# Linear attention mixed with a two-dimensional DFT on one core: transposes in pairs of q' tiles, and operand forms made at other places

## The chip, the cores and the metric

The kernel runs on 1 core of one Trainium2 chip. The metric is the device time of one execution in microseconds (us); the time before is the median of 3 runs. TensorE is called PE, its weight load PEld, VectorE DVE, ScalarE ACT, GpSimd POOL and SyncE SP, as in the profile.

## The reference

Everything is fp32, with S = 2048 rows and D = 576 columns in H = 32 heads of 18.

```python
def _A_ref(x, wqkv, wo):                       # linear attention
    q, k, v = (x @ wqkv) split into three, each into 32 heads
    phi = lambda t: where(t > 0, t + 1, exp(t)) + 1e-6
    pq, pk = phi(q), phi(k)
    kv  = einsum("bhsd,bhse->bhde", pk, v)
    z   = einsum("bhsd->bhd", pk)
    num = einsum("bhqd,bhde->bhqe", pq, kv)
    den = einsum("bhqd,bhd->bhq", pq, z)[..., None] + 1e-6
    return (num / den) joined to (1, S, D) @ wo

def _B_ref(x, dft_seq_re, dft_seq_im, dft_hid_re, dft_hid_im):
    a = x @ dft_hid_re.T ; b = x @ dft_hid_im.T
    return dft_seq_re @ a - dft_seq_im @ b

g = sigmoid((x * gate_w).sum(-1, keepdims=True))
out = g * _A_ref(x) + (1 - g) * _B_ref(x)
```

## The kernel before

**Products.** Every fp32 operand is split into a `hi` and a `lo` part (`hi_of` on ACT, L173, rounds; `lo_of` on DVE, L183, takes the difference), and a product is three matmuls: hi·hi, hi·lo, lo·hi. The last 64 of the 576 columns ("the rest") are packed with their lo into one set of 128 partitions, so a tile of 128 rows against 288 columns takes 14 matmuls, and both halves 28.

**Stages, in PE's order.** (1) k': x times Wk, 16 tiles of 128 rows; the first four run together, the other twelve one after another (`k_half`, L203). The features phi are made by ACT (exp) and DVE (L367), and k' is kept split as `pk`. (2) k'^T x (L676): 20 steps of up to 24 matmuls, each step on one chunk of `xg`, a copy of x in another layout, loaded by SP into a ring of 4 buffers (`cs_ring`, L578) and split by ACT and DVE. After every fourth step `kv_step` (L658, L661) multiplies by Wv. (3) q': 16 tiles (`q_tile`) of x times Wq, which also give the gate's logit; DVE makes the features into `acc[i]`, and 1 + exp(−logit) is inverted with two DVE operations of 128x1 for each tile (L736, L737). Between them M = kv·Wo is built (`build_m`, `split_m`), and `normalise` divides each pair of tiles by its denominators (L749 to L757) and copies the rest columns twice beside each other (`twice`, L762). (4) The attention loop: each normalised tile is transposed by PE, four times 128x128 of `acc` and once `twice` (`transposed`, L779), the transposes are split by ACT and DVE out of PSUM into `qs`, and 28 matmuls (L203) with M give the tile, which ACT evicts with the gate as scale (L1164). (5) The DFT along D (L945) and along S (L1099) in two rounds, each made of seven products of a fast scheme.

**Operand forms for the DFT.** The seven products need sums and differences of blocks of x (left sides) and of the hidden DFT matrix (right sides). `Left(k, ...)` loads a block pair of x (L383, or L389 for the last, k = 8) over POOL's DMA queue, `make` takes two DVE additions twice, the hi on ACT, the lo on DVE, and stores to `xm` in HBM (L408). The last left side is kept for six stores of its rest (`store_rest`, SP). `right(wr, ...)` does the same for three pieces of Wr: load (L435), eight additions on DVE in two steps, hi on ACT (128x2016), lo on DVE (128x1152 and 128x864), store to `wm`. All of this is cut into generators, and `go(gen, n)` puts the next n steps at a chosen place.

**What sets the order.** ACT, DVE and SP run in the order in which the program writes their instructions, from k' on (`manual_schedule`). POOL is ordered by the scheduler, and so is PE until the hidden DFT begins. The tiles of x for k' and q' come by SP into a ring (`load_next`) and are split by `split_next` two tiles ahead. PSUM has 8 banks.

Of the kernel before, what the change touches and what calls it, by code (L numbers as in the profile page):

```python
# [78 lines left out]


PRODUCTS = {1: (4, 0), 6: (2, 4), 2: (6, 1), 5: (1, 3), 7: (0, 5), 3: (3, 2), 4: (5, 6)}
ORDER = (3, 2, 7, 6, 1, 4, 5)
# [49 lines left out]
def kernel(  # L132
# [108 lines left out]

    acc = [at(ACC_AT + i * D * 4, [P, D], F, "acc") for i in range(NT)]

# [130 lines left out]
    class Left:  # L374
# [3 lines left out]
        def __init__(self, k, start, after):  # L378
            self.k = k
            if k < NP:  # L380
                self.f, self.c = (at(start, [P, 7, 2, 2 * P], d, "xb") for d in (F, R))
                for i in range(2):
                    begin_after(nc.gpsimd.dma_start(out=self.f[:, 4 * i + 1:4 * i + 3, 1],  # L383
                                                    in_=xq[k, :, 2 * i:2 * i + 2]), after)
                return
            raw, self.plain = (at(start, [P, 2, 2, 7, P], d, "xb") for d in (F, R))
            self.f, self.c = (t.rearrange("p g a f n -> p f a g n") for t in (raw, self.plain))
            for i in range(4):
                begin_after(nc.gpsimd.dma_start(  # L389
                    out=self.f[:, (1, 2, 5, 6)[i], 1],  # L390
                    in_=xq[k, :, i].rearrange("p (g n) -> p g n", g=2)), after)

# [22 lines left out]
    def store_rest():  # L415
        t = rest_stores.pop()
        for k in range(3):
            for g in range(2):
                nc.sync.dma_start(out=xrest_of[g, k], in_=t[:, g, k // 2])

    def left_part():
# [159 lines left out]
    def xg_next(lo_of=lo_of):  # L581
        if xg_raw:
# [6 lines left out]
            xg_split.append(t)  # L589

    for i in range(FT, NT):
        xs = split.pop(0)
        k_half(i, 0, xs)
        if FT < i < NT - 2:
# [9 lines left out]
        if 8 <= i < 12:  # L604
            xg_load()
        if i < NT - 1:
            load_next()
# [59 lines left out]
    for c in range(5):  # L667
        ps = [bank(), bank()]
        passes = FULL if c < KC else FULL[:2]
        for q in range(NCU):  # L670
# [13 lines left out]
            if step in (1, 2):  # L684
                split_next(lo_later)
            if q == 1 and c:
# [5 lines left out]
            if step == 0:  # L692
                add(zacc, acc[0], acc[1])
            elif step < NT - 1:
                add(zacc, zacc, acc[step + 1])
            if step == NT + 1:
# [20 lines left out]
        gt = gts[c] = at(gt_ring.next(), [P, 2, D], R, "gt")  # L717
# [7 lines left out]
    def q_tile(i):  # L725
        xs = split.pop(0)
        if i == 0:
            split_next()
# [7 lines left out]
        nc.vector.tensor_scalar(g, g, 1.0, None, op0=ALU.add)  # L736
        nc.vector.reciprocal(out=g, in_=g)  # L737
        load_next()
        if i:
            split_next()  # L740

    pz_ring = Ring(T_AT + 40960, D * 4, 4)

    def normalise(k):
# [10 lines left out]
        for i in range(2):  # L755
# [6 lines left out]
            nc.vector.tensor_copy(out=twices[-1],  # L762
                                  in_=rest.unsqueeze(1).to_broadcast([P, 2, REST]))
            yield

    twices = []
    norms = (part for k in range(NT // 2) for part in normalise(k))


    qs_ring = Ring(T_AT + 50176, XS, 2)  # L770

    def transposed(i):

        xs, _ = new_xs("qs", qs_ring)
        banks = [bank(), bank()]
        twice = twices.pop(0)
        for c in range(5):
            a = acc[i][:, c * P:(c + 1) * P] if c < KC else twice.rearrange("p a b -> p (a b)")
            nc.tensor.transpose(banks[c // KC][:, (c % KC) * P:(c % KC + 1) * P], a, ident)  # L779
        hi_of(xs[:, 0:4], banks[0])  # L780
        lo_of(xs[:, 5:9], banks[0], xs[:, 0:4])
        hi_of(xs[:, 4], banks[1][:, :P])
        lo_of(xs[:, 9], banks[1][:, :P], xs[:, 4])
        return xs

# [5 lines left out]
    mraw = at(T_AT + 23040, [P, KC, D], F, "mraw")  # L791
    mrest = at(T_AT + 32256, [P, D], F, "mraw")

    def build_kv():
# [40 lines left out]
    def split_m(h):  # L835
        hi_of(mhi[:, :KC, half(h)], mraw[:, :, half(h)])
        lo_of(mlo[:, :, half(h)], mraw[:, :, half(h)], mhi[:, :KC, half(h)])
        hi_of(mhi[:, KC, half(h)], mrest[:, half(h)])
        lo_of(mhi[64:, KC, half(h)], mrest[64:, half(h)], mhi[64:, KC, half(h)])

    def m_row(h, j):
        return mhi[:, j, half(h)] if j <= KC else mlo[:, j - 5, half(h)]

    store_rest()
    wr_forms, wr_pieces = right(wr, wr_rest, ((0, T_AT + 60416), (1, T_AT + 76544),
                                              (2, T_AT + 60416)))
    xs_ring.at[3] = T_AT + 105664
    load_next()
    q_tile(0)
    for f in wo_split:  # L850
        f()
    kv_step(4)
    q_tile(1)
    build_kv()
    q_tile(2)
    next(norms)
    q_tile(3)
    go(wr_pieces[0])
    next(norms)
    build_m((0, 1))  # L860
    for i in range(4, NT):
        q_tile(i)
        build_m({4: (2, 3), 5: (4,)}.get(i, ()))
        for g in range(2 * (i - 4), min(2 * (i - 3), NG)):
            move_m(g)
        for k, j, n in ((0, 4, 2), (0, 5, 1), (0, 6, 2), (1, 4, 1), (1, 7, 2), (1, 8, 1),
                        (1, 11, 2), (2, 9, 1), (2, 13, 2), (2, 14, 1)):
            if i == j:
                go(wr_pieces[k], n)
        if i in (5, 8, 11, 12, 13):  # L870
            go(norms)
        if i == NT - 3:
            nxt = transposed(0)
        if i in (9, 10):
            split_m(i - 9)

# [182 lines left out]
    def sequence(m, g, src, dst, last=None, between=None):  # L1059
# [91 lines left out]
    made = {}  # L1151
    plan = {
        2: [(0, 1)], 3: [(0, 1)], 4: [(0, 1)], 5: [(0, 1)], 6: [(0, 1)], 7: [(1, 1)], 8: [(1, 1)],
        9: [(1, 1)], 10: [(1, 1)], 11: [(1, 1)], 12: [(7, 1)], 13: [(7, 1)], 14: [(7, 1)],
        15: [(7, 2)],
    }
    for i in range(NT):
        qs = nxt
        if i + 1 < NT:
            nxt = transposed(i + 1)  # L1160
        for h in range(2):
            ps = bank()
            run(ps[:, :HALF], steps(qs, lambda j: m_row(h, j)))
            done.append(nc.scalar.activation(acc[i][:, half(h)], ps[:, :HALF], AF.Copy,  # L1164
                                             scale=gate[:, i:i + 1]))
        nc.gpsimd.dma_start(out=att[i], in_=acc[i])
        go(norms, 2)
        if i == 0:
            go(wr_pieces[2], 2)
        for k, n in plan.get(i, ()):  # L1170
            go(made[k], n)
        for k, j, o in ((0, 0, SLOT_AT), (1, 3, SLOT_AT + 7 * XF),
                        (NP - 1, 8, T_AT + (NP - 2) * TPAIR)):
            if i == j:
                left = Left(k, o, done[-1])
                made[k] = left.make()
                if k < 2:
                    hidden.take_x(k, left.c)
        if i == 7:
# [4 lines left out]
        for p, j in ((1, 8), (2, 11), (3, 15)):  # L1184
            if i == j:
                hidden.load_rest(p)
        if i == 11:
            hidden.load_pair(2)
        if i in (13, 15):
            for k in (0, 2) if i == 13 else (4, 6):  # L1190
                hidden.load_x(3, k)
    nc.vector.tensor_scalar(gate_n, gate, -1.0, 1.0, op0=ALU.mult, op1=ALU.add)
# [34 lines left out]

    paced.enter_context(tc.manual_schedule(engines={mybir.EngineType.PE}))
    first.load_rest(4)
# [96 lines left out]
```

## Time and profile before

| | |
|---|---|
| median of 3 runs | 726.98 us (726.65 to 727.15) |
| the profiled execution | 726.5 us, span 724.8 us |
| granted TensorE clock | 1.0 throughout |
| busy: PE, DVE, ACT, POOL | 719.7, 600.5, 334.7, 57.2 us |
| chain that ended last | PE 94%, DMA 3%, DVE 1% |
| HBM | 115.05 MB read, 41.39 MB written, 216 GB/s |

Stages by PE's timeline, in us of the span: k' until 64.5, k'^T x until 129.5, q' until about 195 (the first transposes are at 183.6), the attention loop until 262.8, hidden DFT until 314.8, sequence DFT until 491.9, the second round until 718, and a tail until 724.8.

How to read the rows: the busy rows give us, share of the span and number of instructions; a group's row has "busy, mean ns of one" and the idle time before its instructions with what ended it; a chain's row has its start, its length and what it is; in a timeline's row stand start and length of a run of instructions and, in brackets, the idle time before it. L numbers are lines of the kernel before.

### The profile page before, as it was taken

Reading aid. Unit: us, or ns where it says so; the run is one execution under the profiler, and the core shown is the slowest. Engines: PE = TensorE matmul, PEld = TensorE weight load, DVE = VectorE, ACT = ScalarE, POOL = GpSimd, SP = SyncE. Lnnn points to the kernel's source line nnn. Section 1 sums busy time; section 2 is a strip of 40 time slices with the busy share of each in tenths; the row PEclk is TensorE's granted clock in tenths of the full one; section 3 lists DMA queues with packets and bytes.
Section 4 is the critical chain, followed back from the end, with each engine's and each line's share of the span. In section 5 each row is a group of like instructions: output and inputs, shape, how many; then the busy total and the mean of one; then the engine's idle time right before and its main releaser. Section 6 shows DMA issues by size and latency. Waiting matters only on the chain.

```text
span 724.8 us, 13886 instructions
## 1 busy us (share of the span) xinstructions
PE 719.7 (99%) x5444; PEld 718.8 (99%) x5444; DVE 600.5 (83%) x995; ACT 334.7 (46%) x522; POOL 57.2 (8%) x98
## 2 busy tenths in 40 slices
PE   9999999999999999999999999999999999999998
PEld 9999999999999999999999999999999999999997
DVE  5789867689999948989999999767889987788884
ACT  5998335688644444543433334323535432232231
POOL 1011300051032210000010000000000000000000
PEclk9999999999999999999999999999999999999999
DMA  7376795676477989744475576889963543454440
GB/s 256 88 276 220 267 338 174 245 218 223 158 218 296 352 311 375 243 158 127 144 265 187 164 280 205 291 307 398 376 219 134 171 154 131 124 178 153 153 153 33
DMA packets 54372, 158.82 MB, mean 219 GB/s; under 512 B 6436, under 2 KB 11108, under 8 KB 53284
## 3 DMA queue, kind: packets, MB, share of 16 engines
q1 hardware_dynamic: 45060, 118.90, 48.6%
q0 software_dynamic: 8960, 38.65, 14.6%
q8 instruction: 43, 0.70, 0.4%
q10 hardware_dynamic: 288, 0.39, 0.1%
q14 instruction: 21, 0.17, 0.1%
HBM read 115.05 MB, written 41.39 MB: 216 GB/s over the span
## 4 chain that ended last, share of the span: by engine, by line
PE 94%; DMA 3%; DVE 1%; POOL 0%; ACT 0%; issue 0%; SPq 0%; DVEq 0%; ACTq 0%; POOLq 0%
PE bank L1099 48%; PE bank L203 23%; PE bank L945 14%; PE bank L676 3%; PE bank L520 2%; PE bank L779 1%; DMA craw<-in_xg_dram 1%; DMA xm<-xb 1%; DMA wraw<-in_wv_dram 1%; PE bank L229 1%; POOL xb L389 0%; PE bank L658 0%; ACT xb L173 0%; DVE row L1115 0%; SPq L311 0%
## 5 line engine op out<-in xcount | busy, mean ns | idle before, releaser
L1099 PE MATMUL bank<-fh,c 128*128 128x288 f32 x1792 | 354.7, 294 | 0.0
L1099 PEld LDWEIGHTS bank<-fh,c 128*128 128x128 f32 x1792 | 286.7, 188 | 0.0
L1099 PE MATMUL bank<-fl,c 128*128 128x288 f32 x896 | 263.6, 294 | 0.0
L173 ACT ACTIVATE c<-craw 128x1792 fp32r<-128x1792 f32 (+1 forms) x84 | 121.3, 1448 | 181.4 <-DVE craw L193 153.6
L1099 PEld LDWEIGHTS bank<-fl,c 128*128 128x128 f32 x896 | 168.7, 188 | 0.0
L183 DVE TENSOR_TENSOR c<-craw,c 128x1792 fp32r<-128x1792 f32 (+4 forms) x86 | 142.0, 1654 | 6.8 <-ACT c L173 6.7
L193 DVE TENSOR_TENSOR craw<-craw 128x256 f32<-128x256 f32 (+1 forms) x192 | 98.0, 512 | 21.4 <-DMA craw<-in_ci_dram 11.5
L203 PE MATMUL bank<-wd,xs 128*128 128x288 f32 (+1 forms) x784 | 105.9, 296 | 0.0
L203 PEld LDWEIGHTS bank<-wd,xs 128*128 128x128 f32 x784 | 104.6, 188 | 0.1
L945 PE MATMUL bank<-wf,xf 128*128 128x288 f32 x588 | 91.1, 295 | 0.0
L945 PEld LDWEIGHTS bank<-wf,xf 128*128 128x128 f32 x588 | 83.4, 189 | 0.0
L203 PE MATMUL bank<-mw,qs 128*128 128x288 f32 x448 | 63.2, 297 | 0.0
L676 PE MATMUL bank<-pk,c 128*128 128x288 f32 x448 | 61.2, 296 | 0.3 <-ACT c L173 0.3
L676 PEld LDWEIGHTS bank<-pk,c 128*128 128x128 f32 x448 | 59.9, 189 | 0.7 <-ACT c L173 0.5
L203 PEld LDWEIGHTS bank<-mw,qs 128*128 128x128 f32 x448 | 59.9, 188 | 0.2 <-DVE qs L183 0.2
L367 DVE SCALAR_TENSOR_TENSOR acc<-bank,e 128x288 f32<-128x288 f32 x64 | 28.2, 453 | 20.1 <-ACT e L366 14.9
L193 DVE TENSOR_TENSOR ys<-bank,ys 128x288 f32<-128x288 f32 x63 | 28.8, 457 | 15.5 <-PE bank L1099 12.5
L183 DVE TENSOR_TENSOR fl<-fl,fh 128x864 fp32r<-128x864 f32 (+1 forms) x32 | 34.5, 1093 | 6.5 <-ACT fh L173 5.3
L173 ACT ACTIVATE fh<-fl 128x864 fp32r<-128x864 f32 (+1 forms) x32 | 29.8, 950 | 16.6 <-DVE fl L193 15.4
L945 PE MATMUL bank<-wf,xr 96*128 96x288 f32 x112 | 33.3, 298 | 0.0
L1164 ACT ACTIVATE acc<-bank,gate 128x288 f32<-128x288 f32 x32 | 16.0, 502 | 35.1 <-PE bank L203 34.8
L193 DVE TENSOR_TENSOR ys<-ys,bank 128x288 f32<-128x288 f32 x47 | 21.2, 450 | 13.3 <-PE bank L1099 12.8
(107 smaller groups left out, 664.6 us busy)
## 6 DMA issues: line engine op xcount, KB each, us to landing
xf<-xm SPq DMA_DIRECT2D x42, 512.0 KB, 9.0
craw<-in_cr_dram SPq DMA_DIRECT2D x32, 512.0 KB, 3.7
craw<-in_ci_dram SPq DMA_DIRECT2D x32, 512.0 KB, 3.7
xraw<-in_xa_dram SPq DMA_DIRECT2D x28, 320.0 KB, 3.9
xm<-xb POOLq DMA_DIRECT2D x8, 1024.0 KB, 6.7
wf<-wm SPq DMA_DIRECT2D x14, 576.0 KB, 5.3
xr<-xr SPq DMA_DIRECT2D x14, 448.0 KB, 8.5
xm<-xb POOLq DMA_DIRECT2D x8, 768.0 KB, 6.7
```

The lines of the kernel that those rows point to most:

```text
L173: return nc.scalar.activation(dst, src, AF.Copy, bias=bias)
L183: nc.vector.tensor_tensor(out=dst, in0=src, in1=hi, op=ALU.subtract)
L193: nc.vector.tensor_tensor(out=dst, in0=a, in1=b, op=op)
L203: nc.tensor.matmul(ps, a, b, start=(n == 0), stop=(n == len(pairs) - 1))
L229: nc.tensor.matmul(warm[:, :P], ones_f, ones_f, start=True, stop=True)
L367: nc.vector.scalar_tensor_tensor(dst, ps, 0.0, e, op0=ALU.max, op1=ALU.add)
L520: nc.tensor.matmul(ps[i][h], x[:, i * P:(i + 1) * P], wkt.row(h, j), start=(c == 0 and n == 0), stop=(c == KC and n == 1))
L676: nc.tensor.matmul(ps[h][:, :HALF], t[:, a, k], pk[s][:, b, half(h)], start=(s == 0 and n == 0), stop=(s == NT - 1 and n == len(passes) - 1))
L779: nc.tensor.transpose(banks[c // KC][:, (c % KC) * P:(c % KC + 1) * P], a, ident)
L945: nc.tensor.matmul(ps, a, b, start=(start and n == 0), stop=(n == len(ops) - 1), skip_group_check=True)
L1099: nc.tensor.matmul(ps[q], c[x][:, l, k], factors[p](y, f), start=(p == 0 and i == 0), stop=(p == NP - 1 and i == 2))
L1164: done.append(nc.scalar.activation(acc[i][:, half(h)], ps[:, :HALF], AF.Copy, scale=gate[:, i:i + 1]))
```

## The change

1. `transposed` now takes a pair of tiles: 4 transposes of 128x128 for each, and one for the rest columns of both (`last`, one copy per pair instead of `twice` for each). Of that last bank, each tile's 64 rows go as hi by ACT to their own partitions and as lo by DVE to the other 64; M's rest has its lo in a tile of its own, `mlast`, 128 partitions wide. The matmuls stay 28 for each tile. PE follows the written order from the attention loop on.
2. The gate's two operations are done once over 128x16, ahead of the attention loop.
3. q' runs in the order `TURNED`: x tiles 12, 13, 14 first, whose splits are kept from k', then 15, 0, 1 to 11. Three loads of x and three splits go.
4. Piece 1 of Wr is made during k' (tiles 4 to 11), piece 0 during k'^T x (steps 13 to 19), piece 2 during q'.
5. x's sides: left side 7 is made between q' tiles 6 and 15 instead of in the attention loop, sides 0 and 1 start one iteration later, and the last left side (8) is loaded by SP at step 6 of k'^T x, into another place; its rest stores go out two at a time after q' tiles 0, 1 and 2. The sum of k' over the tiles (`zacc`) runs from the last tile to the first.
6. `xg` has 5 buffers, and step 0 of k'^T x issues two loads.
7. The norms run earlier among the q' tiles, and loads for the hidden DFT in the attention loop stand at other iterations.

```diff
-            for i in range(4):
-                begin_after(nc.gpsimd.dma_start(
-                    out=self.f[:, (1, 2, 5, 6)[i], 1],
-                    in_=xq[k, :, i].rearrange("p (g n) -> p g n", g=2)), after)
+                nc.sync.dma_start(out=self.f[:, (1, 2, 5, 6)[i], 1],
+                                  in_=xq[k, :, i].rearrange("p (g n) -> p g n", g=2))
...
-    order += list(range(FT, NT)) + list(range(NT))
+    order += list(range(FT, NT)) + TURNED[KEPT:]
...
+    cs_ring.at.append(Y_AT)
...
+        if i in (4, 7, 8, 9, 10, 11):
+            go(wr_pieces[1])
...
-            xg_load()
+            for _ in range(2 if step == 0 else 1):
+                xg_load()
...
-            for k, j, o in ((6, 2, SLOT_AT + 15104), (NP, 6, ACC_AT)):
+            for k, j, o in ((6, 2, SLOT_AT + 15104), (NP, 6, ACC_AT + 22528)):
...
+            if step in (13, 15, 16, 17, 18, 19):
+                go(wr_pieces[0])
...
-            g = gate[:, i:i + 1]
+            g = gate[:, TURNED[i]:TURNED[i] + 1]
...
-        nc.vector.tensor_scalar(g, g, 1.0, None, op0=ALU.add)
-        nc.vector.reciprocal(out=g, in_=g)
...
-            twices.append(at(T_AT + 36864 + (2 * k + i) % 8 * 512, [P, 2, REST], F, "twice"))
-            rest = acc[2 * k + i][:, KC * P:]
-            nc.vector.tensor_copy(out=twices[-1],
-                                  in_=rest.unsqueeze(1).to_broadcast([P, 2, REST]))
+            if i == 1:
+                lasts.append(at(last_ring.next(), [P, 2, REST], F, "last"))
+                nc.vector.tensor_copy(out=lasts[-1], in_=acc_pairs[k][:, :, KC * P:])
...
+    def transposed(k):
+        both = [at(qs_ring.next(), [P, 9, P], R, "qs") for _ in range(2)]
+        mains = [bank(), bank()]
+        last = bank()[:, :P]
+        for i in range(2):
+            for c in range(KC):
+                cs = slice(c * P, (c + 1) * P)
+                nc.tensor.transpose(mains[i][:, cs], acc[2 * k + i][:, cs], ident)
+        nc.tensor.transpose(last, lasts.pop(0).rearrange("p a b -> p (a b)"), ident)
+        for i, t in enumerate(both):
+            hi_of(t[:, 0:4], mains[i])
+            lo_of(t[:, 4:8], mains[i], t[:, 0:4])
+        for i, t in enumerate(both):
+            mine, other = ((slice(0, REST), slice(REST, P))[j] for j in (i, 1 - i))
+            hi_of(t[mine, 8], last[mine])
+            lo_of(t[other, 8], last[mine], t[mine, 8])
+        return both
...
+    early = {4: [(norms, 2)], 5: [(norms, 1), (wr_pieces[2], 1)],
...
-        if i == 0:
-            go(wr_pieces[2], 2)
...
+    nc.vector.tensor_scalar(gate, gate, 1.0, None, op0=ALU.add)
+    nc.vector.reciprocal(out=gate, in_=gate)
...
+        if i % 2 and i + 1 < NT:
+            queue += transposed(i // 2 + 1)
         for h in range(2):
             ps = bank()
-            run(ps[:, :HALF], steps(qs, lambda j: m_row(h, j)))
+            run(ps[:, :HALF], m_steps(qs, h))
```

PE in the attention loop, before: the transposes of one tile, then the matmuls of the tile before it (`mw` is M, `qs` a split tile, `ident` the identity; numbers tell one buffer from another).

```order
L203 MATMUL bank<-mw_1727,qs_2545 128x288 x3
L779 MATMUL bank<-ident_62,acc_89 128x128 x4
L779 MATMUL bank<-ident_62,twice_2543 128x128
L203 MATMUL bank<-mw_1727,qs_2657 128x288
L203 MATMUL bank<-mw_1728,qs_2657 128x288
```

PE there, after: the transposes of a pair, ahead of the matmuls of the second tile of the pair before.

```order
L205 MATMUL bank<-mw_1736,qs_2681 128x288
L787 MATMUL bank<-ident_62,acc_89 128x128 x8
L788 MATMUL bank<-ident_62,last_2675 128x128
L205 MATMUL bank<-mw_1732,qs_2682 128x288
L205 MATMUL bank<-mw_1733,qs_2682 128x288
```

Ten transposes for two tiles have become nine, and they stand at every second tile.

SP in the middle of k'^T x, before (`craw` is a chunk of xg, `wraw` a weight):

```order
L637 DMA wraw_1202<-in_wv_dram 128x576
L578 DMA craw_1234<-in_xg_dram 128x512
L578 DMA craw_1274<-in_xg_dram 128x512
L578 DMA craw_1315<-in_xg_dram 128x512
L309 DMA wraw_1326<-in_wq_dram 128x4x290
L311 DMA wraw_1327<-in_wq_dram 128x290
L578 DMA craw_1355<-in_xg_dram 128x512
```

SP there, after:

```order
L648 DMA wraw_1198<-in_wv_dram 128x576
L582 DMA craw_1230<-in_xg_dram 128x512
L392 DMA xb_1239<-in_xq_dram 128x2x128 x4
L582 DMA craw_1270<-in_xg_dram 128x512
L582 DMA craw_1311<-in_xg_dram 128x512
L312 DMA wraw_1322<-in_wq_dram 128x4x290
L314 DMA wraw_1323<-in_wq_dram 128x290
L582 DMA craw_1351<-in_xg_dram 128x512
```

The four loads of the last left side (`xb`, L392) have come in, and each row of xg stands for the chunk that came one row later before. Those four were on POOL, before:

```order
L383 DMA xb_1082<-in_xq_dram 128x2x256 x2
L389 DMA xb_1243<-in_xq_dram 128x2x128 x4
L408 DMA xm_108<-xb_872 128x2048
L408 DMA xm_108<-xb_872 128x1536
L408 DMA xm_109<-xb_1083 128x2048
```

POOL there, after:

```order
L386 DMA xb_1079<-in_xq_dram 128x2x256 x2
L410 DMA xm_100<-xb_872 128x2048
L410 DMA xm_100<-xb_872 128x1536
L410 DMA xm_101<-xb_1080 128x2048
L410 DMA xm_101<-xb_1080 128x1536
```

The stores of side 5 (`xm`) follow directly on the loads of side 6.

DVE in the attention loop, after, for one pair (before, each tile had one lo of 128x512, one of 128x128 and one copy):

```order
L765 SCALAR_TENSOR_TENSOR acc_90<-acc_90,den_2736 128x576 x2
L770 COPY last_2780<-acc_90 128x128
L185 TENSOR_TENSOR qs_2782<-bank,qs_2782 128x512
L185 TENSOR_TENSOR qs_2783<-bank,qs_2783 128x512
L185 TENSOR_TENSOR qs_2782<-bank,qs_2782 64x128
L185 TENSOR_TENSOR qs_2783<-bank,qs_2783 64x128
L757 SCALAR_TENSOR_TENSOR pz_2838<-acc_91,zb_967 128x576
```

The four lo's of a pair now stand together, and the norm of a later pair (`pz`) follows on them.

More of the change, by code (lines that the diff above doesn't have):

```diff
@@ L78 @@
 LAY_Q = dict(xs=(-256, 4864, 9984, 43776), hi=(15104, 20864), lo=(26688, 31296))
+KEPT = 3
+TURNED = [(i - KEPT - 1) % NT for i in range(NT)]
 PRODUCTS = {1: (4, 0), 6: (2, 4), 2: (6, 1), 5: (1, 3), 7: (0, 5), 3: (3, 2), 4: (5, 6)}
@@ L240 @@
     dens = Ring(small_at[0], 2 * H * 4, 2)
-    acc = [at(ACC_AT + i * D * 4, [P, D], F, "acc") for i in range(NT)]
+    acc_pairs = [at(ACC_AT + k * XD, [P, 2, D], F, "acc") for k in range(NT // 2)]
+    acc = [t[:, i] for t in acc_pairs for i in range(2)]
     raws, split = [], []
@@ L692 @@
             if step == 0:
-                add(zacc, acc[0], acc[1])
+                add(zacc, acc[NT - 1], acc[NT - 2])
             elif step < NT - 1:
-                add(zacc, zacc, acc[step + 1])
+                add(zacc, zacc, acc[NT - 2 - step])
             if step == NT + 1:
@@ L759, in normalise @@
                                            op0=ALU.add, op1=ALU.mult)
-            twices.append(at(T_AT + 36864 + (2 * k + i) % 8 * 512, [P, 2, REST], F, "twice"))
-            rest = acc[2 * k + i][:, KC * P:]
-            nc.vector.tensor_copy(out=twices[-1],
-                                  in_=rest.unsqueeze(1).to_broadcast([P, 2, REST]))
+            if i == 1:
+                lasts.append(at(last_ring.next(), [P, 2, REST], F, "last"))
+                nc.vector.tensor_copy(out=lasts[-1], in_=acc_pairs[k][:, :, KC * P:])
             yield
-    twices = []
+    lasts, last_ring = [], Ring(T_AT + 92672, 2 * REST * 4, 3)
     norms = (part for k in range(NT // 2) for part in normalise(k))
[L770 to L784, printed above, removed]
+    qs_ring = Ring(T_AT + 46592, 9 * P * 4, 3)
+    def transposed(k):
[15 more added lines that the diff above has]
+        return both
     kvb = at(C_AT, [GW, NG, 2, GW], R, "kvb")
@@ L792 @@
     mrest = at(T_AT + 32256, [P, D], F, "mraw")
+    mlast = at(T_AT + 32256, [P, D], R, "mw")
     def build_kv():
@@ L838, in split_m, with m_steps @@
         hi_of(mhi[:, KC, half(h)], mrest[:, half(h)])
[L839 to L847, printed above, removed]
+        lo_of(mlast[:, half(h)], mrest[:, half(h)], mhi[:, KC, half(h)])
+    def m_steps(qs, h):
+        for c in range(KC):
+            yield qs[:, c], mhi[:, c, half(h)]
+            yield qs[:, c], mlo[:, c, half(h)]
+            yield qs[:, 4 + c], mhi[:, c, half(h)]
+        yield qs[:, 8], mhi[:, KC, half(h)]
+        yield qs[:, 8], mlast[:, half(h)]
+    rest_of_x = store_rest()
+    xs_ring.at[3], xs_ring.n = T_AT + 34560, KEPT
     load_next()
     q_tile(0)
+    go(rest_of_x)
     for f in wo_split:
```

78 lines of the change are left out of this document (40 added, 38 removed).

## The prediction

> **What bounds the kernel now.** I began with the page: busy time, then the slices of 1/40 of the span (18.1 us each).
>
> ```profile
> PE 719.7 (99%) x5444; PEld 718.8 (99%) x5444; DVE 600.5 (83%) x995; ACT 334.7 (46%) x522; POOL 57.2 (8%) x98
> ...
> DVE  5789867689999948989999999767889987788884
> ```
>
> PE is the bound of nearly the whole span: 724.8 − 719.7 leaves 5 us of idle, most of it the start and the tail. So a change can only win PE work that disappears, or stalls hidden inside "busy". DVE is full (digit 9) in slices 10 to 14, 163 to 254 us: the late q' tiles and the attention loop. (It is full again in slices 19 to 25, in the sequence transform, which the change leaves alone.) Next, the chain of waits, where one stall of the k'^T x stage stands:
>
> ```profile
> 90.36 6.98 DMA xm<-xb
> ...
> 97.43 0.38 SPq L309
> ...
> 99.85 7.89 DMA craw<-in_xg_dram
> ...
> 107.82 0.64 ACT c L173
> ```
>
> SP, which issues in written order, stands at Wq's load (L309) until a store of x's left side (xm) has landed at 97.4; the chunk of xg behind it goes out at 99.85 and lands at 107.7. What PE loses by it is read from PE's timeline around two equal stretches:
>
> ```profile
> 84.59 13.02 PE L676 MATMUL bank<-pk,c 128*128 128x288 f32 x96
> 97.45 0.28 PE L658 MATMUL bank<-gt,plain 128*126 128x252 f32 x1
> ...
> 98.42 9.82 PE L676 MATMUL bank<-pk,c 128*128 128x288 f32 x72
> ...
> 112.51 0.28 PE L658 MATMUL bank<-gt,plain 128*126 128x252 f32 x1
> ```
>
> 96 matmuls from 84.59 to 97.45 are 0.134 us each; the 100 from 98.42 to 112.51 take 14.09 where 100 × 0.134 = 13.40. **Lost: 0.69.** The same comparison in the q' tiles' end and the attention loop, from the chain:
>
> ```profile
> 184.18 7.57 PE bank L203 x56
> ...
> 203.45 0.55 PE bank L779 x5
> 204.00 3.71 PE bank L203 x28
> ...
> 250.84 3.97 PE bank L203 x28
> ```
>
> 28 matmuls normally take 3.71, so 56 take 7.42 to 7.43; the piece at 184.18 lost **0.14**, the one at 250.84 lost **0.26**. At both DVE's qs came late.
>
> **The change part by part.** *Transposes.* Nine per pair instead of ten: 72 for 80.
>
> ```profile
> L779 PE MATMUL bank<-ident,acc 128*128 128x128 f32 x64 | 9.6, 272 | 0.0
> ```
>
> A mean of 272 ns would make the eight worth 8 × 0.272 = 2.18, but five in a row take 0.55 in the chain and the next matmul starts at once, so one is worth 0.109: **8 × 0.109 = 0.87**. The 28 matmuls per tile stay 28. The bounds are 0.87 and 2.18; I take 0.87, since the chain's row is the elapsed time. The Trainium skill ("TensorE: Matmul & The Clock Gate", Part 4) gives about 275 ns for a transpose in a kernel, which agrees with the mean of one; taken as the price it would make the sum 1.3 us larger.
>
> *The stall at 108.* What held the store is on POOL:
>
> ```profile
> 85.40 2.17 POOL L389 DMA_DIRECT2D xb<-in_xq_dram  x3 [2.42 <-DVE xb L183]
> ...
> 89.80 1.12 POOL L408 DMA_DIRECT2D xm<-xb  x2
> ```
>
> Four loads of the last left side (L389) stand ahead of the store. After the change SP makes them, so the store can go at 85.4 rather than 89.8, 4.4 us earlier; and the fifth xg buffer with two loads at step 0 puts every chunk one step (24 × 0.134 = 3.2 us) earlier in SP's order. Either alone covers 0.69. What it costs: the four loads now stand on SP ahead of two xg chunks. SP's issue cost for that shape does not show; SP's piece at L309 is 0.38, POOL's for three such loads 2.17, so 1.5 to 2.9 us, within the 3.2 won; I take 0. **Gain 0.69, at worst 0.**
>
> *DVE in the q' tiles and the attention loop.* What leaves and joins, by DVE's groups up to 263 us:
>
> ```profile
> L183 DVE TENSOR_TENSOR qs<-bank,qs 128x128 fp32r<-128x128 f32 x16 | 4.5, 281 | 0.0
> L762 DVE COPY twice<-acc 128x128 f32<-128x128 f32 x16 | 3.8, 238 | 0.6
> L193 DVE TENSOR_TENSOR wb<-wb 128x288 f32<-128x288 f32 x8 | 3.5, 455 | 0.1
> L183 DVE TENSOR_TENSOR wb<-wb 128x1152 fp32r<-128x1152 f32 x2 | 2.7, 1354 | 0.0
> L737 DVE RECIPROCAL gate<-gate 128x1 f32<-128x1 f32 x16 | 2.6, 165 | 0.5
> L736 DVE TENSOR_SCALAR gate<-gate 128x1 f32<-128x1 f32 x16 | 2.3, 144 | 0.0
> L183 DVE TENSOR_TENSOR wb<-wb 128x864 fp32r<-128x864 f32 x2 | 2.1, 1053 | 0.0
> ```
>
> Pieces 0 and 1 of Wr leave the q' tiles: 3.5 + 2.7 + 2.1 = 8.3. The gate's 32 small ones become two over 128x16: 4.9 less some 0.4. Half the copies go: 1.9. The small lo's stay 16 in number on 64 partitions; I keep their 4.5. Together 14.7 us of DVE work leave a stretch (131 to 263) in which the two stalls sum to 0.40; three more parts of the norms and Left 7 only move forward inside it. **Gain 0.40, at worst 0.**
>
> Also the rest stores no longer stand ahead of q' tile 0. DVE waited there:
>
> ```profile
> 136.85 0.82 DVE L367 SCALAR_TENSOR_TENSOR acc<-bank,e 128x288 f32<-128x288 f32 x2 [5.12 <-ACT e L365]
> ```
>
> PE did not stop at it, so it counts nothing by itself; DVE merely starts the full stretch with less to catch up.
>
> *Where the pieces go.* Piece 1's steps join the k' tiles, piece 0's the k'^T x stage. The two stretches by windows (the length, then busy time of PE, PEld, DVE, ACT, POOL), and the hi of a piece on ACT:
>
> ```profile
> 31.00:54.00 23.00, 23.00 (x176) 23.00 (x175) 18.77 (x34) 21.23 (x44) 2.60 (x4) 1.00 0.72 246
> 64.50:129.50 65.00, 64.73 (x494) 64.33 (x494) 51.33 (x85) 32.91 (x57) 9.16 (x14) 1.00 0.73 253
> L173 ACT ACTIVATE wb<-wb 128x2016 fp32r<-128x2016 f32 x2 | 3.8, 1880 | 0.0
> ```
>
> One piece is half of 8.3, 4.15 us. In the k' tiles 4.2 is free between 31 and 54, just enough; in k'^T x 13.7 is free, and two xs lo's leave. ACT has 1.8 free there for a hi of 1.9. So the doubt is k', where DVE must hand PE the lo of x two tiles ahead:
>
> ```profile
> 19.85 44.76 PE L203 MATMUL bank<-wd,xs 128*128 128x288 f32 x336
> ...
> 40.36 0.82 DVE L183 TENSOR_TENSOR xs<-xraw,xs 128x640 fp32r<-128x640 f32 x1
> ...
> 43.36 0.82 DVE L183 TENSOR_TENSOR xs<-xraw,xs 128x640 fp32r<-128x640 f32 x1
> ...
> 46.17 0.82 DVE L183 TENSOR_TENSOR xs<-xraw,xs 128x640 fp32r<-128x640 f32 x1
> ```
>
> The twelve tiles take 3.72 each. The lo made at 40.36 to 41.18 belongs to the tile that starts at 20.0 + 6 × 3.72 = 42.3, and lo is first read by the third matmul, 0.27 later: it leads by 1.4. The next lo (43.36) leads by 2.1 in the same way. The piece's first two adds cost 2 × 0.40 = 0.8 of the first lead, and four cost 1.6 of the second: 0.6 and 0.5 remain. The hi on ACT comes two tiles on, where the lead has grown to 3.0 (the lo made at 46.17 for the tile at 49.8), so it stays over 1. I cost it at 0; if DVE runs 1 us later than counted there, PE loses 0.5. The piece's transfers, a load of some 0.6 MB and a store of 2 MB, come on top of 246 GB/s at a DMA share of 0.72 in that window, over 23 us another 110 GB/s; room is there, not much. SP's first load of Wv has to wait for that store; were it 2 or 3 us late, the xg chunks behind it would be less than a step late: 0.
>
> Piece 0 lies in acc of tiles not yet written, so q' tile 2's feature on DVE waits for its store:
>
> ```profile
> wm<-wb POOLq DMA_DIRECT2D x4, 864.0 KB, 8.1
> ```
>
> The last column is the median from issue to landing. Issued at about 130, when k'^T x ends, the store lands by 138; the first half of q' tile 2 is out at 129.5 + 2 × 3.72 + 1.86 = 138.8 at the earliest, and PE, which puts each half into another bank, would feel a late feature only some three halves on, past 144. Cost 0, up to 0.6 if the store goes out 7 us late.
>
> *The new wait.* In the pair's small rest ACT and DVE share one bank: ACT's second hi (64x128) waits for DVE's first small lo, and DVE's second for that hi. Behind the hi on ACT stand two evictions of the attention tiles, and behind the lo on DVE stands the next pair's pz. One pair on DVE now:
>
> ```profile
> 206.17 0.76 DVE L757 SCALAR_TENSOR_TENSOR acc<-acc,den 128x576 f32<-128x576 f32 x1
> ...
> 210.28 0.75 DVE L193 TENSOR_TENSOR xb<-xb 128x256 f32<-128x256 f32 x2
> 210.95 0.88 DVE L183 TENSOR_TENSOR qs<-bank,qs 128x512 fp32r<-128x512 f32 x2
> ...
> 214.13 0.76 DVE L757 SCALAR_TENSOR_TENSOR acc<-acc,den 128x576 f32<-128x576 f32 x1
> ```
>
> 7.96 us, of which 0.67 is x's sides: 7.29, against PE's 2 × (0.55 + 3.71) = 8.52. After: 7.29 less one copy (0.24, of which some 0.14 shows start to start), plus 0.35 for the hand-over (one small operation, 0.28 by DVE's row, and two hops, an estimate), is 7.50; with 0.25 as an upper bound for three starts (the two small lo's and the pz behind them) that no longer overlap the end before them by 0.08, as the adds above do (0.75 together, the next 0.67 later), 7.75. PE takes 9 × 0.109 + 7.42 = 8.40, so DVE's lead grows by 0.65 a pair where no side of x is made. A side costs DVE this:
>
> ```profile
> L183 DVE TENSOR_TENSOR xb<-xb,xb 128x1024 fp32r<-128x1024 f32 x9 | 11.0, 1222 | 7.9 <-ACT xb L173 7.9
> L183 DVE TENSOR_TENSOR xb<-xb,xb 128x768 fp32r<-128x768 f32 x9 | 8.6, 954 | 0.1
> ```
>
> with four adds, 1.22 + 0.95 + 4 × 0.34 = 3.5. From the order I put the lead at the first pair of the loop at 2.1; four pairs on it is 2.1 + 4 × 0.65 − 3.5 = 1.2 at the tenth tile, its smallest. Hidden, cost 0.
>
> A rule of the Trainium skill speaks against this: "VectorE: DVE Perf Modes", section "Two Vector instructions with no wait between them", says that an instruction whose operands start in another group of 32 partitions than the last one's starts only when all earlier ones have finished. The lo's from one half of the partitions to the other would be such. By the rule a pair takes 7.75 and the lead falls to 1.2; without it a pair takes 7.50 and the lead stays near 2.2; the sum is the same by both, and no row of this trace shows such a pair.
>
> **The sum.** 0.87 + 0.69 + 0.40 = 1.96. The profiled execution took 726.5 (span 724.8 and 1.7 around it); 726.5 − 1.96 = 724.5. The median of the runs, 726.98, lies 0.5 above it, so 726.98 − 1.96 = **725.0**.
>
> **The rivals.** *A stall stays or is replaced by its like.* The next late transfer takes the place of xg's: 0.69 stays, 725.7; or the attention lead runs out by 0.8: 725.8; with none of the three stalls gone, 726.1; with k' losing 0.5 and the wait on piece 0's store 0.6 on top, 727.2. For it: DVE's k' lead of 0.5 is thin, and SP's order holds four loads more. Against: two covers for xg, and 14.7 us less on DVE.
>
> *Slower: the hand-over in the attention loop.* DVE's and ACT's queues wait for each other once a pair, ACT with evictions behind the waiting hi, DVE with the pz from which the next transposes come. One eviction is
>
> ```profile
> L1164 ACT ACTIVATE acc<-bank,gate 128x288 f32<-128x288 f32 x32 | 16.0, 502 | 35.1 <-PE bank L203 34.8
> ```
>
> If each hand-over costs e more than counted, the five pairs up to the tenth tile lose 5e − 1.2: nothing below e = 0.24, and slower than the bound below from e = 0.84 (726.98 − 1.56 + 5e − 1.2, without the 0.40). With two evictions in between, e = 1.0: 726.98 − 1.56 + 3.8 = 729.2. For it: DVE is full there. Against: the hi's stand directly behind each other in the order, evictions after them, and DVE gains 14.7.
>
> *The transposes are worth their whole mean.* 8 × 0.272 = 2.18 in place of 0.87: 723.7. Against: the 0.55 in the chain.
>
> **How the numbers follow.** A measurement of this kernel tells 0.2% (1.45 us) from no change: faster is below 725.53, slower above 728.43. The forecast has 0.55, the stall that stays 0.26, the hand-over 0.14, the dear transposes 0.05. Of the forecast and the dear transposes nearly all is faster: 0.60. The stall that stays is within the bound: 0.26. The hand-over is slower: 0.14. The range leaves the hand-over out and takes in the others, 723.6 to 727.2.
>
> **What would show it.** Right: 72 transposes and 0.97 or 0.98 for nine in the chain; no xm and no xg in the chain, and 100 matmuls of k'^T x within 13.4 everywhere; 28 matmuls at 3.71 in all attention tiles; Wq's load released some 4 us earlier. Wrong: PE's k' stretch of 336 above 44.8 (piece 1 too dear); PE idle on DVE's feature at 139 to 146 (piece 0's store); attention tiles above 3.8, with ACT's 64x128 waiting for DVE (the hand-over); PE waiting for c in k'^T x (SP's loads).

## The result, and the profile after

| | before | after |
|---|---|---|
| median, 19 runs each | 727.03 us (725.95 to 730.51) | 725.77 us (724.76 to 726.80) |
| ratio of after to before | | 0.9979, 95% interval 0.9971 to 0.9987 |
| the profiled execution | 726.5, span 724.8 | 726.26, span 724.5 |

Faster by 1.3 us (by the ratio 1.5), where 2.0 was forecast: 725.77 for 725.0, inside the range and just short of what counts as faster. The profiled execution is one of the slower ones of after, only 0.24 below that of before, so its stages say more than its span. From the page of after, the busy rows and DVE's slices:

```profile
PE 718.9 (99%) x5436; PEld 717.8 (99%) x5436; DVE 594.1 (82%) x954; ACT 331.4 (46%) x519; POOL 54.2 (7%) x94
...
DVE  5799687687999828989999999767889988788884
```

PE has 8 instructions fewer, DVE is 6.4 us less busy, and slices 10 to 14 are still nearly full (7, 9, 9, 9, 8). From PE's timeline of after, the k'^T x stage:

```profile
84.85 7.15 PE L687 MATMUL bank<-pk,c 128*128 128x288 f32 x52
92.83 6.12 PE L687 MATMUL bank<-pk,c 128*128 128x288 f32 x44 [0.83 <-DVE c L185]
...
99.76 13.02 PE L687 MATMUL bank<-pk,c 128*128 128x288 f32 x96
...
113.59 10.88 PE L687 MATMUL bank<-pk,c 128*128 128x288 f32 x80
```

The stall at 108 is gone: 96 matmuls from 99.76 take 13.02 as they should. A new one stands at 92, with DVE's lo of a chunk as the releaser. DVE's timeline of after tells what held it:

```profile
87.58 0.75 DVE L195 TENSOR_TENSOR zacc<-zacc,acc 128x576 f32<-128x576 f32 x1
90.62 1.55 DVE L195 TENSOR_TENSOR xb<-xb 128x256 f32<-128x256 f32 x4 [2.29 <-DMA xb<-in_xq_dram]
92.10 0.68 DVE L185 TENSOR_TENSOR c<-craw,c 128x512 fp32r<-128x512 f32 x1
```

DVE stands 2.29 us for the load of x's side 6, makes its four additions, and only then comes to the chunk's lo that PE needs. That load and the store ahead of it, by POOL's timeline of after:

```profile
75.27 0.56 POOL L410 DMA_DIRECT2D xm<-xb  x1 [2.12 <-DVE c L185]
84.61 1.46 POOL L386 DMA_DIRECT2D xb<-in_xq_dram  x2 [8.79 <-ACT xb L175]
```

and of before:

```profile
75.02 0.56 POOL L408 DMA_DIRECT2D xm<-xb  x1 [3.35 <-DVE c L183]
81.50 1.48 POOL L383 DMA_DIRECT2D xb<-in_xq_dram  x2 [5.93 <-DMA xm<-xb]
```

Side 6 is loaded into the buffer of side 4, so it waits until side 4's store has landed, 6.5 us after the store's issue before and 9.3 after. (The row of after names ACT, which was done 0.7 us earlier. In all 14 traces the load follows the last packet on POOL's queue by 1.1 to 1.3: that packet ends at 80.4 before, and at 83.4 after.)

What made that store late stands further up on the same queue. POOL's timeline of after:

```profile
56.52 0.77 POOL L457 DMA_DIRECT2D wm<-wb  x1 [0.68 <-DVE acc L370]
...
71.10 1.47 POOL L386 DMA_DIRECT2D xb<-in_xq_dram  x2 [8.63 <-ACT c L175]
```

and of before:

```profile
65.65 1.47 POOL L383 DMA_DIRECT2D xb<-in_xq_dram  x2 [5.10 <-ACT e L366]
```

Piece 1's store (wm) goes out shortly ahead of side 3's, and the queue's packets then run from 56.4 to 70.0 without a pause over 0.7; before, side 3's store alone runs from 58.0 to 64.5. Side 5's load reuses side 3's buffer and follows its last packet by 1.0 to 1.2 (in ten traces), so it goes out 5.4 us later than before and shares the queue with side 4's store: together they run from 73.2 to 83.4, where side 4's store alone ran from 73.0 to 80.4.

The attention loop by PE's timeline of after:

```profile
207.77 1.03 PE L787 MATMUL bank<-ident,acc 128*128 128x128 f32 x8
208.64 0.27 PE L788 MATMUL bank<-ident,last 128*128 128x128 f32 x1
208.67 7.67 PE L205 MATMUL bank<-mw,qs 128*128 128x288 f32 x56
216.18 1.03 PE L787 MATMUL bank<-ident,acc 128*128 128x128 f32 x8
...
233.89 8.05 PE L205 MATMUL bank<-mw,qs 128*128 128x288 f32 x56
```

A pair takes 216.18 − 207.77 = 8.41, as forecast (8.40). The pair at 233.89 is 0.38 longer and the next one 0.15: DVE's lead, the time by which its lo is ready before PE reads it, has run out there.

Since executions differ in stages that the change does not touch, I compare stages by the starts of their first matmuls in PE's timeline (us):

| kernel, one execution each | first four k' tiles | other k' | k'^T x | q' and attention | the last two |
|---|---|---|---|---|---|
| before | 15.21 | 44.59 | 65.03 | 133.15 | 198.17 |
| before, again | 15.99 | 44.59 | 65.13 | 133.11 | 198.24 |
| after | 15.48 | 44.59 | 65.34 | 132.41 | 197.75 |
| after, second | 15.27 | 44.59 | 64.26 | 132.37 | 196.63 |
| after, third | 15.23 | 44.59 | 64.26 | 132.41 | 196.67 |
| small hi's first | 15.49 | 44.59 | 65.02 | 131.87 | 196.89 |
| side 6 later | 15.73 | 44.59 | | | 196.81 |
| both edits | 15.49 | 44.59 | | | 196.28 |
| both edits, again | 16.19 | 44.59 | | | 196.28 |
| piece 1 among the q' tiles | 15.53 | 44.59 | 64.14 | 134.21 | 198.35 |
| POOL load and ring of 4 | 15.79 | 44.59 | 68.02 | 132.37 | 200.39 |
| POOL load alone | 15.92 | 44.59 | 66.99 | 132.34 | 199.33 |
| ring of 4 alone | 15.73 | 44.59 | 64.84 | 132.39 | 197.23 |
| transposes twice | 15.27 | 44.59 | 65.19 | 138.86 | 204.05 |

(With side 6 later, the scheduler puts some q' matmuls among k'^T x, so only the sum compares.)

### The profile page after: what moved, and what is told of

Its sections match the earlier page's. It is cut to its first block, busy times and chain, and to the rows that moved or that the text cites. A ratio compares the mean times of both kernels' runs of the same rounds, so it can differ in the third digit from the quotient of the medians.

```text
span 724.5 us, 13792 instructions
## 1 busy us (share of the span) xinstructions
PE 718.9 (99%) x5436; PEld 717.8 (99%) x5436; DVE 594.1 (82%) x954; ACT 331.4 (46%) x519; POOL 54.2 (7%) x94
## 4 chain that ended last, share of the span: by engine, by line
PE 83%; DVE 9%; ACT 4%; issue 2%; DMA 2%; POOL 0%; DVEq 0%; ACTq 0%; POOLq 0%
PE bank L1123 48%; PE bank L969 14%; PE bank L205 12%; PE bank L687 5%; PE bank L523 2%; DMA xb<-in_xq_dram 2%; DVE qs L185 1%; DVE acc L765 1%; ACT e L368 1%; ACT xb L175 1%; DVE pz L757 1%; DVE acc L370 1%; DVE xb L195 1%; DVE den L758 1%; DVE xb L185 1%
## 5 line engine op out<-in xcount | busy, mean ns | idle before, releaser
L185 DVE TENSOR_TENSOR fl<-fl,fh 128x864 fp32r<-128x864 f32 (+1 forms) x32 | 34.5, 1093 | 6.6 <-ACT fh L175 5.3
L195 DVE TENSOR_TENSOR fl<-bank,y 128x288 f32<-128x288 f32 x48 | 21.6, 450 | 15.8 <-PE bank L969 15.8
```

The lines of the kernel that those rows point to most:

```text
L185: nc.vector.tensor_tensor(out=dst, in0=src, in1=hi, op=ALU.subtract)
L195: nc.vector.tensor_tensor(out=dst, in0=a, in1=b, op=op)
```

## The experiments

All but the one of before start from the changed kernel. Ratios are to before on the same chip.

**The changed kernel again** (no edit).

> The changed kernel once more, for a second look at its trace. Theory A: the three gains are there (transposes 0.87, the stall at 108 gone 0.69), but two other waits took their place: in k'^T x DVE stands for the load of x's side 6 (2.3 us) with the lo of a chunk queued behind it, PE loses about 1.0 at 92; in the attention loop DVE's lead runs out and PE loses 0.5 at 238 to 247 (0.40 before). So 725.8 again, ratio 0.998, and both places show again, the first with another size since a store's landing sets it. Theory B: these two are accidents of one profiled execution, and the time went elsewhere: then the places are clean here while the time is the same.

Measured 725.10 us, ratio 0.9977 (0.9967 to 0.9986). The two places did not both show. The loss near 237 is there; at 92 nothing, and k'^T x takes 64.26, which I call the clean stage, since no stall is left in it. POOL and DVE of this execution:

```profile
82.86 1.46 POOL L386 DMA_DIRECT2D xb<-in_xq_dram  x2 [7.27 <-ACT xb L175]
```

```profile
88.89 1.55 DVE L195 TENSOR_TENSOR xb<-xb 128x256 f32<-128x256 f32 x4 [2.79 <-DMA xb<-in_xq_dram]
90.36 0.68 DVE L185 TENSOR_TENSOR c<-craw,c 128x512 fp32r<-128x512 f32 x1
```

DVE stands for the load here too, 2.79 us, but the lo comes at 90.4 rather than 92.1, before PE gets there. So theory A holds with one correction: the stall at 92 is 1.08 (65.34 less 64.26) in some executions and nothing in others.

**The changed kernel, a third time.**

> The changed kernel a third time. Theory A: the stall at 92 is there or not by when side 4's store lands (issue of side 6's load before 83: none; at 84.6: 1.1), the loss near 237 is there at 0.4 to 0.55: 725.1 to 725.8.

725.50 us, 0.9979 (0.9971 to 0.9988). Side 6's load at 82.68, no loss at 92, loss at 236.5: as expected. Of the five executions whose k'^T x stage is that of after (three of after, and those with the small hi's first and with the transposes twice), the load came at 82.7 and 82.9 without a loss, and at 83.8, 84.6 and 85.1 with one of 0.8 to 1.1.

**The small hi's first.** In `transposed`:

```diff
+        rows = slice(0, REST), slice(REST, P)
         for i, t in enumerate(both):
-            mine, other = ((slice(0, REST), slice(REST, P))[j] for j in (i, 1 - i))
-            hi_of(t[mine, 8], last[mine])
-            lo_of(t[other, 8], last[mine], t[mine, 8])
+            hi_of(t[rows[i], 8], last[rows[i]])
+        for i, t in enumerate(both):
+            lo_of(t[rows[1 - i], 8], last[rows[i]], t[rows[i], 8])
```

> The two small hi's of a pair are written ahead of the two small lo's, so that ACT's second hi no longer waits for DVE's first small lo. Theory A: DVE's 0.34 of standing in each pair goes, a pair without a side of x takes 7.4 on DVE in place of 7.75, and the lead that ran out at the tenth tile lasts: no loss at 238 and 247, 0.5 faster than the changed kernel (725.3, ratio to before 0.9972). Theory B (the lead is lost by x's sides alone, 9.2 us a pair): the 0.34 goes and at least 0.3 of the loss stays.

725.15 us, 0.9973 (0.9961 to 0.9984). In the runs this cannot be told from the changed kernel; in the trace it can: q' and attention take 131.87 rather than 132.41, with no gap over 0.24 us left in them. Theory A: DVE's pair, by its timeline, first with the edit:

```profile
201.63 1.92 DVE L185 TENSOR_TENSOR qs<-bank,qs 128x512 fp32r<-128x512 f32 x4
203.58 0.76 DVE L757 SCALAR_TENSOR_TENSOR pz<-acc,zb 128x576 f32<-128x576 f32 x1
...
209.18 1.93 DVE L185 TENSOR_TENSOR qs<-bank,qs 128x512 fp32r<-128x512 f32 x4
```

and in after, with the lo's of the four later pairs:

```profile
202.25 1.59 DVE L185 TENSOR_TENSOR qs<-bank,qs 128x512 fp32r<-128x512 f32 x3
204.19 0.29 DVE L185 TENSOR_TENSOR qs<-bank,qs 64x128 fp32r<-64x128 f32 x1 [0.34 <-ACT qs L175]
204.51 0.76 DVE L757 SCALAR_TENSOR_TENSOR pz<-acc,zb 128x576 f32<-128x576 f32 x1
205.31 0.75 DVE L758 TENSOR_REDUCE den<-pz 128x32 f32<-128x576 f32 x1
205.98 0.75 DVE L757 SCALAR_TENSOR_TENSOR pz<-acc,zb 128x576 f32<-128x576 f32 x1
...
210.09 1.60 DVE L185 TENSOR_TENSOR qs<-bank,qs 128x512 fp32r<-128x512 f32 x3
...
219.27 1.60 DVE L185 TENSOR_TENSOR qs<-bank,qs 128x512 fp32r<-128x512 f32 x3
...
228.24 1.60 DVE L185 TENSOR_TENSOR qs<-bank,qs 128x512 fp32r<-128x512 f32 x3
...
236.70 0.76 DVE L195 TENSOR_TENSOR xb<-xb 128x256 f32<-128x256 f32 x2
237.49 1.60 DVE L185 TENSOR_TENSOR qs<-bank,qs 128x512 fp32r<-128x512 f32 x3
```

With the edit a pair takes 7.55, without it 7.84: the hand-over is 0.3 a pair, and taking it away restores the lead.

**Side 6 later.**

```diff
-            if q < NCU - 1:
+            if q < NCU - 1 and step != 6:
                 left_part()
```

> No step of x's sides is written in step 6 of k'^T x, so that side 6's first additions stand behind the next chunks' lo's on DVE. Theory A: DVE does not stand with a chunk's lo behind it, PE loses nothing at 92: about 0.7 to 1.0 faster than the changed kernel (725.0). Theory B: the next late thing takes its place (the second load of Wq, which waits for side 6's store, then holds SP): no gain, and a loss near 112 to 118.

725.68 us, 0.9983 (0.9974 to 0.9992): no gain in the runs. No gap over 0.24 in k'^T x; the loss at 237 stays. DVE still stands 1.96 us for the load, until 90.16, but with the chunk's lo already done.

**Both edits**, run twice.

> Both edits together. Theory A: the sum, 1.2 to 1.5 faster than the changed kernel: 724.4, ratio to before 0.996, and PE's pace without a gap from 64.7 to 262. Theory B: one of the two only, or neither: 725.2 to 725.8.

> The version with the small hi's first and no part of x's sides in step 6, once more and beside the changed kernel on one chip. Theory A: PE without a gap of over 0.24 from 20 to 262 again, 0.4 to 1.5 below the changed kernel, as that has its stall at 92 in this execution or not: 724.5 to 725.3. Theory B: no difference.

725.35 us, 0.9976 (0.9966 to 0.9985), and 725.52 us, 0.9984 (0.9975 to 0.9993). In both traces the last two stages take 196.28, which is 198.17 − 1.96 = 196.21 to within 0.07: the forecast's sum. In the second execution side 6's load came at 84.90, 64.1 us after PE had begun the tile-by-tile k', and nothing was lost; without the later side, 0.8 was lost at 63.6 (small hi's first) and 1.1 at 64.5 (after). But the hidden DFT takes 52.25 in both traces where it takes 51.98 to 51.99 in every other one, from one place in PE's timeline (that of the second execution):

```profile
299.61 0.29 PE L970 MATMUL bank<-wf,xr 96*128 96x288 f32 x1
299.93 1.06 PE L970 MATMUL bank<-wf,xf 128*128 128x288 f32 x6
```

So 0.35 is won against a clean execution of after and 0.26 given back. It is not faster than the changed kernel by any measurement here: theory B of the second expectation. What PE waits for at 299.9 the trace does not name; it stays open.

**Piece 1 among the q' tiles.**

```diff
-    wr_forms, wr_pieces = right(wr, wr_rest, ((0, ACC_AT + 6144), (1, T_AT + (NP - 1) * TPAIR),
+    wr_forms, wr_pieces = right(wr, wr_rest, ((0, ACC_AT + 6144), (1, T_AT + 60416),
...
-        if i in (4, 7, 8, 9, 10, 11):
-            go(wr_pieces[1])
...
+        go(wr_pieces[1], {4: 1, 7: 2, 8: 1, 11: 2}.get(i, 0))
```

> Piece 1 of Wr made among the q' tiles 4 to 11 (in another place) instead of during k'. Theory A: the piece is what makes DVE and ACT late in k' and fills POOL's DMA queue, so that the store of side 4 lands late and the load of side 6 with it: without it the load of side 6 is issued near 81.5 as before the change, not at 84.6, DVE does not stand for it at 88 to 91, and no loss at 92. In exchange 4.2 us of DVE work come back into the q' tiles, DVE enters the attention loop later, and the loss there grows from 0.4 to 0.5 to between 1 and 3 (PE slower by that). Theory B: SP's loads or the two chunks at step 0 make the loads late: side 6's load stays at 84.

728.77 us, 1.0018 (1.0008 to 1.0029). Theory A in both halves, except that the loss sits in the q' tiles themselves and the attention loop runs without a stall. POOL, and PE's waits from 64 to 263:

```profile
81.53 1.47 POOL L386 DMA_DIRECT2D xb<-in_xq_dram  x2 [6.56 <-DMA xm<-xb]
```

```profile
PE bank L205 <- DVE acc L370: 1.2, 1, 1.2
PE bank L205 <- DVE xs L185: 0.6, 1, 0.6
```

k'^T x is clean at 64.14, and q' with attention takes 134.21, 1.8 more than in after. (The profiled execution took 726.72 where the median is 728.77, so the trace does not show all that the runs lost.) On DVE three lo's of Wr stand together there:

```profile
181.77 4.59 DVE L185 TENSOR_TENSOR wb<-wb 128x1152 fp32r<-128x1152 f32 x3
```

Side 5's load goes out at 64.46 again and side 4's last packet ends at 80.4, as before the change. So the piece in k' is what makes side 6 late, and its price there is well below its price among the q' tiles.

**The last left side on POOL, and xg in a ring of 4**: both undone, then each alone.

```diff
-                nc.sync.dma_start(out=self.f[:, (1, 2, 5, 6)[i], 1],
-                                  in_=xq[k, :, i].rearrange("p (g n) -> p g n", g=2))
+                begin_after(nc.gpsimd.dma_start(
+                    out=self.f[:, (1, 2, 5, 6)[i], 1],
+                    in_=xq[k, :, i].rearrange("p (g n) -> p g n", g=2)), after)
...
-    cs_ring.at.append(Y_AT)
...
-            for _ in range(2 if step == 0 else 1):
-                xg_load()
+            xg_load()
```

> The last left side loaded by POOL again, and xg in a ring of 4 with one load in step 0, as before the change; the rest of the change stays. Theory A: the stall at 108 comes back at 0.5 to 0.8, with SP standing at Wq's load until side 5's store has landed: the time of k'^T x as before the change, 65.0, 0.7 above the clean 64.3. Theory B: the stall at 108 went because other things moved (three loads of x and two splits left the stage): it stays away.

> Only the last left side's load goes back to POOL; xg keeps 5 buffers and two loads in step 0. Theory A (what stops PE in the run with neither is DVE standing for the last left side's load, which came late on POOL's queue, with a chunk's lo behind it): the stall at 104 stays, 1.5 to 2, and the one at 92 too; k'^T x takes 67 to 68. Theory B (the prediction's: either of the two edits alone covers the chunks): 64.3 to 65.3.

> Only xg goes back to 4 buffers with one load in step 0; the last left side stays on SP. Theory A: its four loads on SP, some 4.5 us, now hold the chunks behind them, which are needed 3.2 us sooner after their issue: a loss of 0 to 1 near 100 to 108 beside the one at 92; k'^T x takes 65 to 66. Theory B (the prediction's: either alone covers): 64.3 to 65.3, as with both.

Neither: 729.42 us, 1.0030 (1.0019 to 1.0041). POOL load alone: 727.79 us, 1.0010 (1.0001 to 1.0020). Ring of 4 alone: 725.99 us, 0.9991 (0.9982 to 1.0000). With neither, k'^T x takes 68.02, 3.8 above the clean 64.26, far more than the 0.5 to 0.8 expected: not the old stall came back but another. DVE's and PE's waits of that run (64 to 112 and 64 to 263):

```profile
DVE xb L195 <- DMA xb<-in_xq_dram: 8.6, 3, 4.1
```

```profile
PE bank L687 <- DVE c L185: 3.2, 3, 1.7
```

POOL and DVE with the POOL load alone:

```profile
87.75 0.72 POOL L392 DMA_DIRECT2D xb<-in_xq_dram  x1 [0.76 <-DVE zacc L195]
...
96.70 0.72 POOL L392 DMA_DIRECT2D xb<-in_xq_dram  x1 [2.37 <-issue]
```

```profile
103.32 1.56 DVE L195 TENSOR_TENSOR xb<-xb 128x256 f32<-128x256 f32 x4 [3.45 <-DMA xb<-in_xq_dram]
104.80 0.68 DVE L185 TENSOR_TENSOR c<-craw,c 128x512 fp32r<-128x512 f32 x1
```

POOL issues the four loads 3 us apart, the last at 96.7, and DVE stands for them with a chunk's lo behind it: 2.73 lost (66.99 less 64.26). Of that some 0.5 lies at 92, behind side 6 as in after, and in the run with neither some 1.3 of the 3.8; the rest lies at 104 to 109, behind the last left side. With the ring of 4 alone the loss is 0.58, by ACT standing for a chunk's landing until 108.19; the one at 92 was absent in that execution (side 6's load at 83.25). The stage of 64.84 lies in theory B's range, but the place is theory A's.

**Transposes twice.** In `transposed`, the loop over the eight `acc` transposes is written a second time behind the first.

> Each pair's eight transposes of 128x128 are done twice (64 more in all); nothing else changes. Theory A (a transpose costs PE 0.109, as the chain's rows give it): 64 x 0.109 = 7.0 slower than the changed kernel, 732.3 to 732.7, a pair of tiles at 9.27 instead of 8.40. Theory B (it costs its mean of 0.272): 64 x 0.272 = 17.4 slower, 743. The loss of 0.4 near 238 goes in both, since PE's longer pairs give DVE more time.

732.61 us, 1.0074 (1.0059 to 1.0089). Theory A. PE's timeline:

```profile
209.16 1.03 PE L787 MATMUL bank<-ident,acc 128*128 128x128 f32 x8
210.03 0.27 PE L788 MATMUL bank<-ident,last 128*128 128x128 f32 x1
210.14 1.04 PE L792 MATMUL bank<-ident,acc 128*128 128x128 f32 x8
210.93 7.67 PE L205 MATMUL bank<-mw,qs 128*128 128x288 f32 x56
218.44 1.03 PE L787 MATMUL bank<-ident,acc 128*128 128x128 f32 x8
```

A pair takes 9.28 against 8.41, 0.87 for eight. Over all, 138.86 less 131.87, the stretch without a stall, is 6.99 for 64: 0.109 each.

**Before, again.**

> The kernel before once more, for a second trace. Theory A: k'^T x with the q' tiles and the attention loop takes 198.2 again (stalls 0.69 and 0.40 among it), k' after its first four tiles 44.6, and only the first four tiles, which wait for the first loads, differ from one execution to another (15.2 to 15.7). Theory B: the stall at 108 is an accident of one execution, and the stage is 0.7 shorter here.

726.98 us, 0.9998 (0.9987 to 1.0008). Theory A: 198.24, the stall at 108 there again. The first four tiles took 15.99, just over the span of 15.2 to 15.7 that I gave.

## Why the prediction was right or wrong

**Transposes: right.** 0.109 each, shown by doubling them. The rival with 0.272 each falls; that is how long one is under way, and 0.109 is how far apart they start.

**The stall at 108: gone, as forecast, but not for the reason given.** The stage went from 65.03 to the clean 64.26: 0.77 for 0.69. "Either alone covers 0.69" fell: with SP's loads but a ring of 4 there is 0.58 of loss, with the ring of 5 but POOL's loads 2.73. (In the second of these ACT stands for no chunk from 85 on; PE was late there itself, so whether the fifth buffer alone covers the chunks is not shown.) The working looked at the chunks alone. The last left side's own load decides more: its additions stand on DVE ahead of a chunk's lo. Two sizes were off besides. SP's timeline of after:

```profile
88.67 4.54 SPq L392 DMA_DIRECT2D xb<-in_xq_dram  x4
...
96.31 0.38 SPq L312 DMA_DIRECT2D wraw<-in_wq_dram  x1
```

SP's four loads took 4.1 to 4.5 in the three executions of after, where the working had 1.5 to 2.9 within the 3.2 won, and Wq's load went out 1.1 to 2.4 earlier than at 97.43, not some 4.

**Piece 1 in k': free in k', not free behind it.** k' took 44.59 in every trace, with and without the piece, so the leads of 0.6 and 0.5 sufficed. The step that failed is "I cost it at 0": it followed DVE, ACT and SP, and of POOL's queue only the piece's own store. Behind it on that queue side 3's store, side 5's load and side 4's store each come later, so side 6's load does too, and DVE stands for it in k'^T x. The price is 0 or 0.8 to 1.1 by execution.

**Attention and q': 0.40 forecast, not won.** The stage fell by 0.74, of which the transposes are 0.87; a loss of 0.5 stands where 0.40 stood. The hand-over was sized well (0.35 counted, 0.3 by the edit). The lead was not. "I put the lead at the first pair at 2.1": the trace gives 1.3 (the first lo ends at 202.9, and PE reads it 0.27 after tile 2 starts at 204.0). And "four pairs on it is 2.1 + 4 × 0.65 − 3.5" left out side 1's first additions (236.70, 0.8): from 202.25 to 237.49 DVE took 35.24, where that working has 4 × 7.75 + 3.5 = 34.5 and PE takes 33.6. So 1.3 − 1.6 is below nothing at the tenth tile (counted from 0), the one in which PE stops near 238. The rule of the Trainium skill ("VectorE: DVE Perf Modes", section "Two Vector instructions with no wait between them") agrees with the rows: behind the lo that crosses the partitions, pz starts 0.03 after the end (204.51), while the next pz, behind an ordinary instruction, starts 0.08 before it (205.98). With the small hi's first all three starts of the bound are late like that: the four lo's take 1.92 there, the two large ones 1.28 of it and the small ones 0.28 and 0.29, so each small one starts 0.03 after the end before it, as pz does (203.58). So they cost some 0.33 a pair where the working had 0.25 as the upper bound, and a pair without x's sides took 7.84, above the 7.75 at which it still saw the lead last.

**The rivals.** What happened is a mixture: the forecast in two of three executions of after, less the 0.4 to 0.5 of the attention loop; in the third also "a stall is replaced by its like", with 1.08. 725.0 + 0.5 is 725.5, plus a part of 1.08, against the median of 725.77. So the median lies nearer to that rival's 725.7 and 725.8 than to the 725.0 of the forecast; beside before on the same chip the three medians of after fell by 1.26, 1.98 and 1.05. The range takes this rival in, so it holds either way. The slower rival did not come: the hand-over cost 0.3 a pair over the count without it, not 0.84 over the count with it.

## What to carry to other kernels

When work moves into a stage with idle time on the engine, follow its DMA queue and the buffers behind it too: a store that lands 3 us later delays the load that reuses its buffer, and on an engine in written order everything behind the consumer of that load stands. A lead is worked out by listing every instruction between its two ends, not by a mean per round plus the one extra that comes to mind. When the gains are tenths of a per cent, compare stages between the same two instructions, and profile the same kernel more than once: here one stall was there in one execution of three.

## What the runs showed of the hardware

The first four k' tiles, whose code the change leaves alone, took 15.21 to 16.19 us in 14 traces, and the tiles after them 44.59 in all. Of the 1.3 us between the spans of the two executions of before, the start makes 0.78; of the 1.3 between those of after it makes 0.2, and the stall at 92 makes 1.08. A 128x128 transpose takes 0.27 us and the next starts 0.109 after it, also when 17 follow each other. A side's store of 1.8 MB on POOL's queue, its second part issued at 75.0 to 75.3, had its last packet at 80.4 in before, and at 81.5 to 83.4 in three executions of the changed kernel, with side 5's load ahead of it on the queue.
